# A weight matrix requested earlier and the start of a Fourier-mixing and MLP kernel rearranged around three waits of TensorE

## The chip, the cores and the metric

The kernel runs on one core of one Trainium2 chip. The metric is the device time of one execution in microseconds (us). A profiled execution also gives the span (first to last instruction) and the mean granted clock of TensorE (PE). The span is about 1.8 us shorter than the device time (626.1 against 627.84 us in the profiled run of before).

## The reference, cut to what matters

```python
def _attn_ref(x):                       # x: 8 x 3008 x 256
    X = np.fft.fft(x, axis=1)
    X = np.fft.fft(X, axis=2)
    return X.real.astype(np.float32)

def _moe_ref(x, w_tok1, w_tok2, w_ch1, w_ch2):
    xt = x.transpose(0, 2, 1)
    h = np.maximum(xt @ w_tok1, 0.0) @ w_tok2       # tokens: 3008 -> 256 -> 3008
    u = x + h.transpose(0, 2, 1)
    h2 = np.maximum(u @ w_ch1, 0.0) @ w_ch2         # channels: 256 -> 1536 -> 256
    return u + h2
```

## The kernel before

For each of eight batches the kernel computes the two Fourier transforms as products with generated tables (`fold`, then `z`, `w`, and `y` as the third stage), the token relu (`tok1`), the sum `u` (`tok2`), and the channel MLP (`mm1` with relu, `mm2`). In the traces PE keeps the order in which the kernel emits its instructions, also where it waits: in the changed kernel it idles 0.68 us before a `pw` at 73.32 us, and the two `pc` emitted behind that `pw` start at 73.50. What fills PE while it waits is therefore decided by the order in which the kernel emits work. Python generators give out that work in steps: `take(own, 2)` emits the next two steps of the first batch's front part.

```python
    def filler(n):                      # matmuls whose result nobody reads
        pw = ps_out("filler")
        for _ in range(n):
            nc.tensor.matmul(pw[:, 0:P], lhsT=ident[:], rhs=lrot[:], start=True, stop=True)
    ...
    # the copy of z out of PSUM: copy(1, ...) is VectorE, copy(0, ...) ScalarE
                copy(half == 0 and b > 0 or b == 0 and t0 == 1 and half, zo[:, :, :, t0:t0 + 5], ...)
    ...
        if b == 0:
            yield from rot()
            yield from y(0)
            yield from tok1()           # the token relu uu
            yield from tok2(0)          # pu <- uu, then ut
            for c in (1, 2):
                yield from y(c)
                yield from tok2(c)
    ...
    def mm1(b, c, c1, ct):              # pc <- ut, two halves h
        ...
        for h in range(2):
            nc.tensor.matmul(pc[:, 0:n], lhsT=wc1[:, h, ct * P:(ct + 1) * P],
                             rhs=ut[:, c, h, 0:n], start=(h == 0), stop=(h == 1))
    ...
    take(own, 2)
    take(tu_r, 3)
    filler(8)
    take(own, 2)
    filler(8)
    take(own, 4)                        # z is whole after this
    take(tu_b0, 3)                      # back: pr <- tts, copied by VectorE
    take(tu_b2, 3)                      # back: pr <- tts, copied by ScalarE
    ...
    for k in range(6):
        take(own, 2)                    # two pw
        take(car, 1)                    # one ph <- w1p, w1m
    ...
    NFRONT = 42                         # steps of the next batch's front, spread over the slots
    ...
                while done < NFRONT * (slot + 1 - first) // (71 - first):
                    take(nxt, 1)
                    done += 1
```

The first token matrix is loaded as `w1p` and `w1m` from the POOL queue. It was requested after all generated tables and their memsets, near 10 us.

## Time and profile before

| | before |
|---|---|
| device time, first three runs | 629.15 us (628.19 to 629.95) |
| span of the profiled run | 626.1 us, clock 0.999 |
| PE busy | 609.8 us, 97% |
| PE idle after 44 us, before the last matmul | none that the waits view shows |
| first `prot` / first `po` | 26.32 / 44.95 us |

The page's line of the chain that ended last says who limits the kernel. PE holds 96% of it.

```profile
PE 96%; DVE 2%; DMA 1%; ACT 0%; issue 0%; DVEq 0%
```

The view of PE's waits, longest first, in the kernel before. The columns are: who waited, for whom, us in total, times, longest.

```profile
PE filler L344 <- DVE ident L84: 8.0, 1, 8.0
PE pr L380 <- DVE tts L384: 1.0, 2, 0.8
PE pu L488 <- DVE uu L84: 0.9, 1, 0.9
PE pz L418 <- DVE eo L90: 0.5, 1, 0.5
PE pc L545 <- DVE ut L90: 0.5, 2, 0.3
...
```

The lines shown all lie in the first 37 us. The timeline of PE in the kernel before shows where. The columns are: start, duration, engine, line, operation, result and sources, shapes, count, and the idle time before with its releaser.

```profile
13.51 1.48 PE L371 MATMUL pr<-lrot,tp 128*128 128x128 f16 x12
...
20.04 0.38 PE L380 MATMUL pr<-tts,anti 128*128 128x512 f16 x1 [0.82 <-DVE tts L384]
...
21.32 0.27 PE L442 MATMUL pw<-td,z 128*128 128x257 f16 x1
...
34.60 0.96 PE L488 MATMUL pu<-w2n,uu 128*128 128x512 f16 x3 [0.93 <-DVE uu L84]
35.81 0.38 PE L545 MATMUL pc<-ut,wc 128*128 128x512 f16 x1 [0.26 <-DVE ut L90]
36.41 0.38 PE L545 MATMUL pc<-ut,wc 128*128 128x512 f16 x1 [0.22 <-DVE ut L90]
...
44.95 1.47 PE L575 MATMUL po<-wc,c 128*128 128x256 f16 x12
```

`pw` starts at 21.32 because `back` (`pr`) waits for VectorE's copies. `pu` waits for the token relu. The two halves of the first `pc` wait for the two halves of `ut`.

The table of busy time by window in the kernel before: window, length, busy us and count of PE, PEld, DVE, ACT and POOL, then PE clock, DMA share, GB/s.

```profile
10.00:11.00 1.00, 1.00 (x6) 0.45 (x5) 1.00 (x4) 0.90 (x2) 1.00 (x4) 1.00 1.07 217
11.00:12.00 1.00, 1.00 (x12) 0.93 (x9) 1.00 (x4) 1.00 (x3) 1.00 (x2) 1.00 0.67 53
12.00:13.00 1.00, 0.47 (x6) 0.28 (x5) 1.00 (x5) 1.00 (x2) 1.00 (x3) 1.00 0.86 139
```

The last column falls from 217 to 53 GB/s. The requests for the token rows were nearly served, and those for `w1p` went out only from 10.12 us on, too late to follow without a gap.

### The profile page before, as it was taken

The numbers are of one execution on the slowest core, as the hardware profiler recorded it, in microseconds if no ns is written. First come the engines' busy times: TensorE is split into PE (matmuls) and PEld (weight loads), VectorE is DVE, ScalarE is ACT, GpSimd is POOL, SyncE is SP. The second block draws the span as 40 slices with busy tenths as digits, with TensorE's granted clock in tenths as the row PEclk, the third lists the DMA queues.
The fourth block names the chain that finished last, engine by engine and source line by source line (L and its number), as shares of the span: only waits on it lengthen the run. The fifth ranks groups of instructions, "written<-read, shape, count | busy, mean of one in ns | idle before, by whom it ended". The sixth has DMA issues, their size and how long they took to land.

```text
span 626.1 us, 11728 instructions
## 1 busy us (share of the span) xinstructions
PE 609.8 (97%) x4765; PEld 423.0 (68%) x4765; DVE 343.2 (55%) x730; ACT 291.0 (46%) x571; POOL 170.5 (27%) x231
## 2 busy tenths in 40 slices
PE   4889999999999999999999999999999999999997
PEld 3656676667667676667766776667766677666666
DVE  8768647634664356554665447653466536653343
ACT  8643553554434643365434544356443554344441
POOL 8401890292013900166010850039000000000000
PEclk9999999999999999999999999999999999999999
DMA  8994845428224462426532296242223323332435
GB/s 149 210 157 87 146 81 122 85 60 155 53 52 93 80 135 61 80 52 134 107 69 50 64 153 92 48 94 51 51 52 67 86 51 52 82 68 56 89 64 106
DMA packets 83366, 55.46 MB, mean 89 GB/s; under 512 B 53746, under 2 KB 80050, under 8 KB 82546
## 3 DMA queue, kind: packets, MB, share of 16 engines
q1 hardware_dynamic: 76816, 36.82, 30.0%
q0 software_dynamic: 6176, 17.63, 15.8%
q8 instruction: 37, 0.61, 0.4%
q10 hardware_dynamic: 320, 0.26, 0.2%
q14 instruction: 17, 0.14, 0.1%
HBM read 35.26 MB, written 24.64 MB: 96 GB/s over the span
## 4 chain that ended last, share of the span: by engine, by line
PE 96%; DVE 2%; DMA 1%; ACT 0%; issue 0%; DVEq 0%
PE po L575 39%; PE pc L545 39%; PE pu L488 7%; PE pt L510 3%; PE pz L418 2%; PE py L468 2%; PE pw L442 2%; DMA xm<-in_x_dram,ix 1%; PE pw L444 1%; PE ph L397 0%; PE ph L399 0%; PE filler L344 0%; DVE z L101 0%; DVE ut L90 0%; PE pr L371 0%; DVE eo L90 0%
## 5 line engine op out<-in xcount | busy, mean ns | idle before, releaser
L545 PE MATMUL pc<-ut,wc 128*128 128x512 f16 (+1 forms) x1152 | 306.6, 374 | 0.7 <-DVE ut L90 0.5
L97 ACT ACTIVATE c<-pc 128x512 f16<-128x512 f32 (+1 forms) x384 | 214.2, 587 | 195.8 <-PE pc L545 142.7
L575 PE MATMUL po<-wc,c 128*128 128x256 f16 x2256 | 276.3, 273 | 0.0
L575 PEld LDWEIGHTS <-c 128*128 128x128 f16 x2256 | 220.6, 98 | 63.2
L84 DVE TENSOR_SCALAR c<-pc 128x512 f16<-128x512 f32 (+1 forms) x192 | 129.8, 676 | 98.6 <-PE pc L545 97.8
L545 PEld LDWEIGHTS <-wc 128*128 128x128 f16 x1152 | 103.2, 98 | 69.6 <-issue 4.2
L90 DVE TENSOR_TENSOR osb<-po,uT 128x258 f32<-128x258 f32 (+1 forms) x196 | 71.8, 408 | 125.4 <-PE po L575 122.4
L90 DVE TENSOR_TENSOR ut<-pu,yt 128x512 f16<-128x512 f32 (+1 forms) x96 | 63.6, 672 | 9.7 <-PE pu L488 9.7
L97 ACT ACTIVATE w<-pw 128x257 f16<-128x257 f32 x90 | 34.6, 385 | 50.9 <-PE pw L444 50.9
L90 POOL TENSOR_TENSOR eo<-fa,fb 96x512 f16<-96x512 f16 (+1 forms) x48 | 54.1, 1148 | 0.0
L488 PE MATMUL pu<-w2r,uu 128*128 128x512 f16 (+1 forms) x168 | 50.0, 379 | 0.0
L689 POOL COPY tail<-c 128x768 f16<-128x768 f16 x4 | 3.3, 823 | 170.2 <-ACT c L97 170.2
L687 POOL COPY c<-tail 128x768 f16<-128x768 f16 x4 | 3.3, 823 | 138.9 <-PE po L575 138.9
L90 DVE TENSOR_TENSOR yt<-py,sqy 128x512 f16<-128x512 f32 x48 | 30.9, 685 | 9.5 <-ACT sqy L97 9.5
L488 PEld LDWEIGHTS <-uu 128*128 128x128 f16 x192 | 18.7, 98 | 16.0 <-DVE uu L84 1.3
L90 POOL TENSOR_TENSOR fa<-xp,xm 96x512 f16<-96x512 f16 x24 | 27.5, 1146 | 1.9 <-DMA xm<-in_x_dram,ix 1.9
L101 DVE CAST z<-pz 128x480 f16<-128x480 f32 (+1 forms) x38 | 24.3, 652 | 6.1 <-PE pz L418 5.0
L90 POOL TENSOR_TENSOR fb<-xm,xp 96x512 f16<-96x512 f16 x24 | 27.5, 1146 | 0.0
L97 ACT ACTIVATE z<-pz 128x480 f16<-128x480 f32 x26 | 17.2, 675 | 20.1 <-PE pz L418 19.7
L97 ACT ACTIVATE sqy<-py 128x512 f32<-128x512 f32 x24 | 14.3, 596 | 25.1 <-PE py L468 23.8
L442 PE MATMUL pw<-td,z 128*128 128x257 f16 x96 | 25.6, 273 | 0.0
L90 POOL TENSOR_TENSOR eo<-xp,xm 96x4 f16<-96x4 f16 x24 | 5.2, 217 | 73.0 <-PE pz L432 72.9
(136 smaller groups left out, 338.3 us busy)
## 6 DMA issues: line engine op xcount, KB each, us to landing
out_dram<-osb SPq DMA_DIRECT2D x83, 256.0 KB
xp<-in_x_dram POOLq DMA_DIRECT2D x14, 408.0 KB, 5.2
out_dram<-osb SPq DMA_DIRECT2D x11, 192.0 KB
uT<-ut SPq DMA_TRANSPOSE x96
w2n<-in_moe_w_tok_dram POOLq DMA_DIRECT2D x2, 752.0 KB, 13.2
w1p<-in_moe_w_tok_dram POOLq DMA_DIRECT2D x2, 384.0 KB, 5.4
wc<-in_moe_w_ch_dram POOLq DMA_DIRECT2D x1, 768.0 KB, 16.4
xp<-in_x_dram POOLq DMA_DIRECT2D x2, 272.0 KB
```

The lines of the kernel that those rows point to most:

```text
L84: eng.tensor_scalar(out=out_, in0=in_, scalar1=s1, scalar2=None, op0=op0)
L90: eng.tensor_tensor(out=out_, in0=a, in1=b, op=op)
L97: nc.scalar.activation(out=out_, in_=in_, func=func, scale=scale, **kw)
L101: V.tensor_copy(out=out_, in_=in_)
L418: nc.tensor.matmul(pz[:, 96 * k:96 * k + 96], lhsT=eo[:, t0 + k, c], rhs=t1r, start=True, stop=True)
L442: nc.tensor.matmul(pw[:, 0:257], lhsT=zg[:, 1, g], rhs=td1[:], start=True, stop=False)
L444: nc.tensor.matmul(pw[:, 0:129], lhsT=zg[:, 0, g], rhs=td0[:], start=False, stop=True)
L468: nc.tensor.matmul(py[:, P * k:P * k + P], lhsT=w[:, 4 * c + k, o:o + P], rhs=tab[:, 4 * c + k, :], start=True, stop=True)
L488: nc.tensor.matmul(pu[:, 0:64 * nk], lhsT=uu[:, th, h, :], rhs=w2[:, th, :, 8 * c:8 * c + nk], start=(th == 0), stop=(th == 1))
L510: nc.tensor.matmul(pt[:, o:o + n], lhsT=hw[:, g, c], rhs=w[:, g, w0:w0 + n], start=(g == 0), stop=(g == NG - 1))
L545: nc.tensor.matmul(pc[:, 0:n], lhsT=wc1[:, h, ct * P:(ct + 1) * P], rhs=ut[:, c, h, 0:n], start=(h == 0), stop=(h == 1))
L575: nc.tensor.matmul(po[:, o:o + D], lhsT=c1[:, ct, ks * P:ks * P + P], rhs=wc2[:, ct, :], start=(ct == 0), stop=(ct == NCT - 1))
```

## The change

It has four parts, named by letters from here on.

- **W**: `w1p` and `w1m` are requested right behind the first token rows, from 6.4 us.
- **Z**: `back` is cut up and spread between the `z` steps and the `pw` steps, more `z` copies go to ScalarE, and 12 of 28 fillers go.
- **Y**: the third stage `y` has three steps, and the first two steps of `y(1)` are emitted between the token relu and `tok2(0)`, so that its eight matmuls fill the wait for `uu`. The third step of `y` also raises the number of steps per batch, so `NFRONT` becomes 45.
- **H**: the first three `pc` of the first chunk run all their first halves, then all their second halves.

```diff
+    load_w1p()
     ts(mask[:, 0:1], pcol[:], float(NQ), AT.is_lt, eng=G)
     ts(top[:], pcol[:], float(KR - 1), AT.is_lt, eng=G)
     tt(mask[:, 1:2], xicol[:], top[:], AT.mult, eng=G)
+    load_w1m()
+    (memsets of w1m, e128, td1 moved here too; loads and memsets removed at the old place)
@@ z copies
-                copy(half == 0 and b > 0 or b == 0 and t0 == 1 and half, zo[:, :, :, t0:t0 + 5],
+                copy(half == 0 and b > 0, zo[:, :, :, t0:t0 + 5],
-            copy(1, zo, pz[:, 0:96].rearrange("p (u k) -> p u k", u=4))
+            copy(b > 0 or half, zo, pz[:, 0:96].rearrange("p (u k) -> p u k", u=4))
@@ y
             act(sq[:], ps[1][:])
+            yield
@@ front, b == 0
+            y1 = y(1)
+            next(y1)
+            next(y1)
+            yield
             yield from tok2(0)
-            for c in (1, 2):
-                yield from y(c)
-                yield from tok2(c)
+            yield from y1
+            yield from tok2(1)
+            yield from y(2)
+            yield from tok2(2)
@@ mm1: cts=range(3) for the first call, loops over the three pc inside each half (cut)
@@ order of the start
-    filler(8)
+    filler(4)
     take(own, 2)
-    filler(8)
+    take(tu_b0, 2)
     take(own, 4)
-    take(tu_b0, 3)
-    take(tu_b2, 3)
+    take(tu_b0, 1)
     for k in range(6):
         take(own, 2)
+        take(tu_b2, 1 if 0 < k < 4 else 0)
         take(car, 1)
@@
-    NFRONT = 42
+    NFRONT = 45
```

(The counts of `take(own, ...)` and the slots in `own_at`, which follow from the new steps, are cut.)

More of the change, by code (lines that the diff above doesn't have):

```diff
@@ L158, with load_w1p, load_w1m @@
     tw23, q25 = pvec("tw23"), pvec("q25")
+    def load_w1p():
+        for i in range(2):
+            gdma(w1p[64 * i:64 * i + 64, :, :].rearrange("p (c g) d -> p c (g d)", c=3),
+                 dram(w1_t, 4 * i * DTOK, [[NQ * DTOK, 64], [8 * DTOK, 3], [1, 4 * DTOK]]))
+    def load_w1m():
+        for i in range(2):
+            h = slice(64 * i, 64 * i + 64)
+            n = 3 - i
+            gdma(w1m[h, 0:4 * n, :].rearrange("p (c g) d -> p c (g d)", c=n),
+                 dram(w1_t, (24 + 4 * i) * DTOK,
+                      [[NQ * DTOK, 64], [8 * DTOK, n], [1, 4 * DTOK]]))
+        gdma(w1m[64:128, 8:11, :].rearrange("p g d -> p (g d)"),
+             dram(w1_t, 44 * DTOK, [[NQ * DTOK, 64], [1, 3 * DTOK]]))
     V.memset(tw23[:], TWO23)
@@ L179 @@
     top, acol = pvec("top"), pvec("acol")
+    ixc = const.tile([P, 2], I32, tag="ixc")
+    cfeat = pvec("cfeat")
+    load_w1p()
     ts(mask[:, 0:1], pcol[:], float(NQ), AT.is_lt, eng=G)
@@ L182 @@
     tt(mask[:, 1:2], xicol[:], top[:], AT.mult, eng=G)
-    ixc = const.tile([P, 2], I32, tag="ixc")
-    cfeat = pvec("cfeat")
+    load_w1m()
+    G.memset(w1m[64:128, 11, :], 0.0)
+    G.memset(e128[:], 0.0)
+    G.memset(td1[:, 0:130], 0.0)
+    G.memset(td1[0:1, 0:128:2], 0.5)
+    G.memset(td1[0:1, 1:129:2], -0.5)
     ts(cfeat[:], pcol[:], 1.0, AT.is_ge, 128.0, AT.mult, eng=G)
@@ L271 @@
     sin(td1[:, 130:257], md[:, 129:256])
-    G.memset(e128[:], 0.0)
-    G.memset(w1m[64:128, 11, :], 0.0)
-    G.memset(td1[:, 0:130], 0.0)
-    G.memset(td1[0:1, 0:128:2], 0.5)
-    G.memset(td1[0:1, 1:129:2], -0.5)
-    for i in range(2):
-        gdma(w1p[64 * i:64 * i + 64, :, :].rearrange("p (c g) d -> p c (g d)", c=3),
-             dram(w1_t, 4 * i * DTOK, [[NQ * DTOK, 64], [8 * DTOK, 3], [1, 4 * DTOK]]))
-    for i in range(2):
-        h = slice(64 * i, 64 * i + 64)
-        n = 3 - i
-        gdma(w1m[h, 0:4 * n, :].rearrange("p (c g) d -> p c (g d)", c=n),
-             dram(w1_t, (24 + 4 * i) * DTOK,
-                  [[NQ * DTOK, 64], [8 * DTOK, n], [1, 4 * DTOK]]))
-    gdma(w1m[64:128, 8:11, :].rearrange("p g d -> p (g d)"),
-         dram(w1_t, 44 * DTOK, [[NQ * DTOK, 64], [1, 3 * DTOK]]))
     ts(acol[:], pcol[:], -1.0, AT.mult, 127.0, AT.add, eng=G)
@@ L538, in front, with mm1 @@
                 yield from tok2(c)
-    def mm1(b, c, c1, ct):
+    def mm1(b, c, c1, ct, cts=None):
         ut = state[b]["ut"]
         n = min(CW, S - CW * c)
-        pc = ps_mm("pc")
+        cts = cts or (ct,)
+        pcs = [ps_mm("pc") for _ in cts]
         for h in range(2):
-            nc.tensor.matmul(pc[:, 0:n], lhsT=wc1[:, h, ct * P:(ct + 1) * P],
-                             rhs=ut[:, c, h, 0:n], start=(h == 0), stop=(h == 1))
-        if ct % 3:
-            act(c1[:, ct, 0:n], pc[:, 0:n], func=AFT.Relu)
-        else:
-            ts(c1[:, ct, 0:n], pc[:, 0:n], 0.0, AT.max)
+            for pc, ct in zip(pcs, cts):
+                nc.tensor.matmul(pc[:, 0:n], lhsT=wc1[:, h, ct * P:(ct + 1) * P],
+                                 rhs=ut[:, c, h, 0:n], start=(h == 0), stop=(h == 1))
+        for pc, ct in zip(pcs, cts):
+            if ct % 3:
+                act(c1[:, ct, 0:n], pc[:, 0:n], func=AFT.Relu)
+            else:
+                ts(c1[:, ct, 0:n], pc[:, 0:n], 0.0, AT.max)
     tail1 = const.tile([P, NCT, 64], FP16, tag="tail1")
@@ L637 @@
         take(own, 2)
+        take(tu_b2, 1 if 0 < k < 4 else 0)
         take(car, 1)
-    take(own, 3)
+    take(own, 4)
     take(car, 6)
-    take(own, 4)
+    take(own, 5)
     setup.close()
@@ L645 @@
     w2v[1] = w2r[:]
-    NFRONT = 42
-    own_at = {0: 2, 2: 1, 3: 1, 12: 1, 15: 1, 18: 1, 21: 1, 24: 1, 27: 1, 30: 1, 33: 1,
+    NFRONT = 45
+    own_at = {1: 1, 2: 1, 4: 1, 12: 1, 15: 1, 18: 1, 20: 1, 22: 1, 24: 1, 27: 1, 30: 1, 33: 1,
               36: 1, 39: 1}
@@ L660 @@
                 slot = NCT * c + ct
-                mm1(b, c, c1, ct)
+                if b == 0 and slot < 3:
+                    if slot == 0:
+                        mm1(b, c, c1, ct, range(3))
+                else:
+                    mm1(b, c, c1, ct)
                 if ct == 4:
```

## The prediction

> **What bounds the kernel.** The page gives TensorE 97% busy at a granted clock of 1.0, and the chain of waits is 96% PE. In the table of busy time by window, PE has no idle time from 44 us to the last matmul (622 us); 4.0 us of output DMA follow. So only the first 44 us can be shortened. Of them PE is idle about 12.4 us, 8.0 before anything can run. The rest, from the timeline of PE:
> - 18.8 to 21.3 us: `back` waits for three VectorE copies (2.08 us), which wait behind the stage-one copies `z`; the first `pw` starts at 21.32, although `z` is whole at 19.46.
> - 33.2 to 34.6: `pu` waits for the token relu `uu` (0.93 idle).
> - 35.2 to 36.4: `pc` waits for the two halves of `ut`.
> DMA is saturated near 200 GB/s from 2.3 to 43 us, except 11 to 12.7 us, where it falls to about 0 to 100 GB/s: `w1p` was requested only at 10.1, the token rows were finished.
>
> **What the change does.** No arithmetic is removed but 12 fillers.
> 1. `w1p`, `w1m` requested from about 6.4 instead of 10.1. [...] Missing bytes of the gap at 205 GB/s: 1.0 us (estimate). The last `w1m` piece landed near 21.1 before (second piece 20.6, by landings), so near 20.1.
> 2. `mask` moves behind two DMA issues (1.38 us): ready near 9.2. VectorE needs it for `t1n` and 0.7 us more before the fold; the fold waits for tokens until 9.99 anyway. Delay 0 to 0.4.
> 3. `back` is split and interleaved, both last `z` copies go to ScalarE: `z` whole near 18.7 to 19.2, `pw` starts there, about 2.3 earlier. But `ph` then meets `w1m` at 20.1, and the loop gets 3 `pr` (0.22 each) and 3 ScalarE copies (0.54 each) more: about 5.3 us of PE or 5.1 of ScalarE. `prot` starts near 25.0 instead of 26.32: gain 1.3.
> 4. `y(1)`'s eight matmuls (0.43) fill the wait for `uu`; three first-half `pc` (0.65) fill the wait for the second `ut`. Afterwards VectorE's queue (relu 0.6, `yt` 1.2, `ut` 0.6) rules until `pc` of ct 6: gain 0.8.
> 5. From then on PE is full; the third yield per `y` reorders VectorE work only, with no idle PE to gain or lose: 0.
>
> **Predicted time.** 629.15 - 1.3 - 0.8 = 627.05, say 627.0 us (0.35%), 8 in 10 between 625.2 and 628.7. Over 2% faster would need 12.6 us, more than the start can give: 0.01; over 2% slower 0.01; within 0.98.
>
> **What would show it.** DMA at 11 to 12.7 us near 200 GB/s; first `pw` at 18.7 to 19.3 with a PE wait for DMA `w1m` (to about 20.1) before the first `ph`; `prot` near 25.0; PE wait for `uu` under 0.5; the first `po` near 42.9 instead of 44.95; from there to the end the same length within 0.3 us.
>
> **What would make it wrong.** `w1p` sharing the engines with the second token gather and delaying the fold; [...] ScalarE as new limit of the `pw` loop; run-to-run scatter of 1.8 us, as large as the gain.

Two passages are cut. One gave a rule for the order of transfers in a queue as the reason why `w1p` and `w1m` would run behind the token rows; without it that order was assumption. The other was a risk for which no trace here gives a measure. No term of the forecast goes with them: 629.15 - 1.3 - 0.8 = 627.05. The "near 200 GB/s" is 185 to 212 GB/s in the trace of before, at a busy share of 0.99 to 1.18, over the stretches from 2.3 to 43 us without the gap.

## The result, and the profile after

| | before | changed |
|---|---|---|
| device time, six runs | 628.67 us (627.39 to 630.14) | 626.53 us (626.34 to 628.33) |
| span, changed runs at clock 1.000 | | 624.6, 624.6, 624.7, 624.8 |
| span, changed runs at clock 0.997 | | 626.5, 626.6 |

The ratio is 0.9974, with a 95% interval from 0.9951 to 0.9996. A ratio is worked out from the runs of both kernels, so it is not quite the ratio of the medians. The time lies inside the predicted range, and the medians differ by 2.14 us, as forecast. The table's last two rows already show that this is not the whole story: the six runs of the changed kernel fall in two groups, and the clock sorts them.

The profiled run was one of the slower group. Its waits of PE:

```profile
PE filler L350 <- DVE ident L84: 8.7, 1, 8.7
PE pw L448 <- DVE z L101: 0.7, 1, 0.7
PE pw L448 <- ACT z L97: 0.6, 1, 0.6
...
PE ph L405 <- DMA w1m<-in_moe_w_tok_dram: 0.5, 1, 0.5
...
PE pu L495 <- DVE uv L90: 0.4, 1, 0.4
...
```

Its timeline of PE, in the places shown of before (line numbers have shifted):

```profile
13.84 0.83 PE L377 MATMUL pr<-lrot,tp 128*128 128x128 f16 x12
...
19.17 0.27 PE L448 MATMUL pw<-td,z 128*128 128x257 f16 x1 [0.56 <-ACT z L97]
...
20.50 0.37 PE L405 MATMUL ph<-w1m,tts 128*128 128x256 f16 x1 [0.51 <-DMA w1m<-in_moe_w_tok_dram]
...
34.81 1.29 PE L495 MATMUL pu<-w2n,uu 128*128 128x512 f16 x4 [0.44 <-DVE uv L90]
36.36 1.46 PE L559 MATMUL pc<-ut,wc 128*128 128x512 f16 x6 [0.26 <-DVE ut L90]
...
45.05 1.47 PE L590 MATMUL po<-wc,c 128*128 128x256 f16 x12
```

Four things are as intended: `pw` starts at 19.17 instead of 21.32, `ph` meets `w1m`, the wait of `pu` falls from 0.93 to 0.44 us (and now ends with `uv`, the step before the token relu), and the six `pc` run as one group. Yet the first `po` comes at 45.05, no earlier than before, where 42.9 was predicted. In the table by window the DMA gap is filled, and the PE clock shows the main reason why the gain is missing in this run (besides, VectorE began the fold of the tokens 0.55 us later than in the trace of before, at 10.54 us):

```profile
11.00:12.00 1.00, 1.00 (x7) 0.66 (x6) 1.00 (x4) 1.00 (x3) 0.87 (x5) 1.00 0.99 180
...
16.55:19.96 3.41, 2.15 (x23) 1.41 (x24) 3.31 (x10) 2.77 (x6) 2.33 (x4) 1.00 1.12 206
19.96:23.37 3.41, 2.90 (x16) 2.02 (x15) 0.96 (x3) 1.71 (x4) 2.78 (x4) 0.50 1.15 227
```

From 19.96 to 23.37 us the clock is 0.50, right where the `pw` and `ph` loop runs. The trace of before has no such stretch. It pays in another place: its twelve `pr` at 13.51 take 1.48 us against 0.83 in the changed trace, because PE still ran at a slow rate then. Both traces start at this rate: their first twelve fillers, of the same 128x128 shape, take 1.46 us. It ended where the clock records begin. In the trace of before they begin only at 17.23 us, with the full clock, and ten `pz` take 1.00 us at 15.64 and 0.59 at 17.27; those of the changed kernel begin at 13.13. (They are in the packed traces. The views print 1.00 where there is no record, so the 1.00 in the lines above that end before these times says nothing.)

The third new item is a wait that did not exist before, `pw` for a VectorE copy of `z`, 0.7 us. It is at 73 us, in what was the full part:

```profile
72.40 0.18 PE L433 MATMUL pz<-t1n,eo 96*128 96x24 f16 x1
72.43 0.17 PE L436 MATMUL pz<-cms,e 96*128 96x24 f16 x1
72.45 0.19 PE L438 MATMUL pz<-t1b,eo 96*128 96x72 f16 x1
73.32 0.28 PE L448 MATMUL pw<-td,z 128*128 128x257 f16 x1 [0.68 <-DVE z L101]
```

### The profile page after: what moved, and what is told of

It reads as the page before. It is cut to its first block, busy times and chain, and to the rows that moved or that the text cites. A ratio compares the mean times of both kernels' runs of the same rounds, so it can differ in the third digit from the quotient of the medians. Undisturbed runs are those within 1.5% of the kernel's fastest.

```text
span 626.6 us, 11701 instructions
## 1 busy us (share of the span) xinstructions
PE 608.9 (97%) x4753; PEld 420.9 (67%) x4753; DVE 344.8 (55%) x728; ACT 293.2 (47%) x573; POOL 170.4 (27%) x231
## 4 chain that ended last, share of the span: by engine, by line
PE 95%; DMA 2%; DVE 1%; POOL 1%; ACT 0%; issue 0%; DVEq 0%
PE po L590 39%; PE pc L559 39%; PE pu L495 7%; PE pt L517 3%; PE pw L448 2%; DMA w1m<-in_moe_w_tok_dram 2%; PE py L474 2%; PE pz L424 1%; PE pw L450 1%; PE ph L405 0%; PE ph L403 0%; POOL xm L109 0%; DVE ix L86 0%; POOL w1p L106 0%; POOL w1m L106 0%
## 5 line engine op out<-in xcount | busy, mean ns | idle before, releaser
L97 ACT ACTIVATE z<-pz 128x480 f16<-128x480 f32 (+1 forms) x28 | 18.2, 686 | 26.7 <-PE pz L424 26.7
```

The source lines that it names most:

```text
L97: nc.scalar.activation(out=out_, in_=in_, func=func, scale=scale, **kw)
```

## The experiments

Theory A is the prediction: the four parts shorten the start by 1.3 (W and Z) and 0.8 us (Y and H). To this came two theories from the trace: C, the new wait at 73 us is made by `NFRONT` 45; and D, the half-clock stretch, called the dip from here on, is caused by too little matmul work in the 3.41 us before it, so the kernel can avoid it. (A clock window means such a stretch of 3.41 us from here on. The section on the dip shows where the windows lie.) Their rivals are that the wait is made up elsewhere, and that the dip is chance. Twelve kernels ran, each beside the kernel before on the same chip. All twelve gave correct results. p1 to p4 ran on one chip, p5 to p8 on a second and p9 to p12 on a third. The kernel before took 625.6 to 625.7, 625.5 to 625.7 and 625.4 to 625.6 us on them in its runs at clock 1.000, so a comparison across these groups can be off by about 0.2 us. "Clean" means a run at clock 1.000 or 0.999, "dip" one at 0.997 or lower.

### p1_again: the changed kernel once more

No edit.

> The changed kernel once more, for a second profile and the shares of its runs. Theory A (the start is shorter by the four parts, and a dip of the TensorE clock to half for 3.4 us spoils some runs): runs fall in two groups, span near 624.7 us at a granted clock of 1.000 and near 626.5 us at 0.997, nothing between; in a profile without the dip prot starts near 25.0 to 25.5 and the first po near 43.0. Theory B (the clock in the records is a side matter and the scatter is start-up chance alone): times spread evenly over 2 us and don't go with the clock.

Measured: spans 626.0, 626.2, 626.2, 626.4 at 0.997, and 625.0 at 1.000. The ratio is 0.9996 (0.9983 to 1.0009): in these rounds the change brought nothing, as four of its five runs dipped, and three of the eleven of before. Of these, before had 625.6 to 625.7 in its five runs at 1.000. Its three runs at 0.999 took 626.2 to 626.4, like its profiled run (626.1 at 0.999), which kept the slow rate of the start until 17.23 us. That the three did so too is likely and not shown. They are left out wherever runs at 1.000 are compared. The two groups are confirmed, and the median is set by how many runs dip. No clean profile of the changed kernel was caught; p7 gives one.

### p2_noW: without part W

```diff
-    load_w1p()            # behind the token rows
-    load_w1m()
+    load_w1p()            # at the old place, after the tables
+    load_w1m()
```

> The change without its first part: w1p and w1m requested at their old place, near 10 us. Theory A: first pw still near 18.7 to 19.2, but PE then waits for w1m until about 21.1 to 21.6 before ph can go on (0.5 us with the early request), so it is 0.8 to 1.2 us slower than the changed kernel in runs of the same clock. Rival: the gain comes from the rest alone, and the early request is worth under 0.3 us.

Measured: 625.3 in the one clean run against 624.6 to 625.0 of the changed kernel, four dips (626.1 to 626.9). In the profile, which is of the clean run, PE waited for `w1m` until 20.57 us, not until 21.1 to 21.6 as expected, and the loss is 0.3 to 0.7 us instead of 0.8 to 1.2. One clean run is too little; p10 repeats it without dips.

### p3_noZ: without part Z

```diff
-    filler(4)
+    filler(8)
     take(own, 2)
-    take(tu_b0, 2)
+    filler(8)
     take(own, 4)
-    take(tu_b0, 1)
+    take(tu_b0, 3)
+    take(tu_b2, 3)
@@ and the z copies as before; take(tu_b2, ...) goes from the loop (cut)
```

> The change without the split of back and without the z copies on ScalarE (16 fillers again). Theory A: the first pw starts near 21.3 us as before, no wait for w1m, and it is 1.0 to 1.5 us slower than the changed kernel in runs of the same clock; with 16 fillers the half-clock dip near 20 us does not come. Rival: the w1m landing is the limit anyway, so it is under 0.5 us slower.

Measured: 625.6, 625.6, 625.7 clean, two dips (626.4, 626.7). Against the changed kernel's 624.6 to 625.0, part Z is worth 0.6 to 1.1 us at equal clock, a little less than expected. The first `pw` starts at 20.80. My guess that 16 fillers in their old places prevent the dip was wrong: the profiled run has one from 19.11 us.

### p4_noY: without part Y

```diff
-            y1 = y(1)
-            next(y1)
-            next(y1)
-            yield
             yield from tok2(0)
-            yield from y1
-            yield from tok2(1)
+            yield from y(1)       # after tok2(0), as before; y in two steps, NFRONT 42
+            yield from tok2(1)
```

> The change without y(1) filling the wait for the token relu (and without the third yield of y). Theory A: the wait of pu for uu is 0.9 us instead of 0.44, and it is 0.3 to 0.5 us slower. Rival: VectorE's queue rules until pc of ct 6, so moving 0.43 us of PE work changes nothing: under 0.15 us.

Measured: 625.1, 625.1, 625.2 clean, three dips. The wait for `uu` is 0.92 us again. From `prot` (26.36) to the first `po` (45.38) it takes 19.02 us; the changed kernel takes 18.21 (26.84 to 45.05) and the kernel before 18.63. So Y is worth 0.8 us beside H, and H alone makes this stretch 0.4 longer. The total loses less than 0.8, as this kernel doesn't have the new wait at 73 us: from the first `po` to the end it takes 581.1 us, like before, and the changed kernel 581.5.

### p5_noH: without part H

```diff
-                if b == 0 and slot < 3:
-                    if slot == 0:
-                        mm1(b, c, c1, ct, range(3))
-                else:
-                    mm1(b, c, c1, ct)
+                mm1(b, c, c1, ct)
```

> The change without the first chunk's halves apart. Theory A (prediction): pc of the first half has no more work to fill the wait for the second half of ut, 0.3 to 0.4 us slower in runs at the same clock. Rival: VectorE's queue rules up to ct 6, so at most 0.1 us. Seen before: from prot to the first po 18.63 us in the kernel before, 18.21 with both parts, 19.02 with the halves apart but no filled relu wait; this run gives the fourth corner.

Measured: `prot` (26.27) to the first `po` (44.43) 18.16 us, against 18.21 with H. Clean spans 624.7 and 624.8, no difference; the other four runs dipped (625.9 to 626.5). The fourth corner is in: neither 18.63, Y alone 18.16, H alone 19.02, both 18.21. Part H is worth nothing beside Y, and alone it costs 0.4.

### p6_pace: the extra step of y only where it is used

```diff
             act(sq[:], ps[1][:])
-            yield
+            if b == 0:
+                yield
@@
-    NFRONT = 45
+    NFRONT = 42
```

> The changed kernel with y's third yield only for the first batch and NFRONT 42 again. Theory C: the third yield set NFRONT to 45, the first batch then takes its eighth and ninth step in one slot, and pw waits 0.7 us for the z copy (seen near 73 us in all four kernels with 45, not in the two with 42); so this wait goes, the stretch from the first po to the end falls from 581.5 to 581.1 us, and runs at the same clock are 0.3 to 0.5 us shorter. Rival: the wait is made up elsewhere, no difference.

Measured: the wait is gone. PE's timeline of this kernel at the same place has the two `pc` back between `pz` and `pw`:

```profile
72.08 0.19 PE L438 MATMUL pz<-t1b,eo 96*128 96x72 f16 x1
72.11 0.60 PE L560 MATMUL pc<-ut,wc 128*128 128x512 f16 x2
73.02 0.27 PE L448 MATMUL pw<-td,z 128*128 128x257 f16 x1
```

From the first `po` (44.68) to the end (625.8) it takes 581.1 us instead of 581.5, as theory C asks. The dipping runs are 625.6 to 626.0 against 625.9 to 626.6 of the changed kernel and p5. The one clean run is 624.5. The cause can be counted from the code: of the steps of the next batch that are taken during the first batch, step 8 is the last `pz` and step 9 the first `pw`. With 45 steps over 40 slots, the floor of 45·n/40 is 7 at n = 7 and 9 at n = 8, so both fall in one slot with no `pc` between them; with 42 it is 8 and then 9.

### p7_fill: fillers in the waits of the start

```diff
     take(tu_b0, 2)
-    take(own, 4)
+    filler(4)
+    take(own, 1)
+    filler(4)
+    take(own, 1)
+    filler(4)
+    take(own, 2)
     take(tu_b0, 1)
+    filler(8)
```

> The changed kernel with 20 fillers put into the waits of PE between 16 and 19.2 us. Theory D: the half-clock stretch of 3.4 us that starts between 19.1 and 20.0 in the dipping runs comes from a window with too little matmul work before it (0.7 to 1.34 us of columns in 3.41 us); the fillers add 1.07 us, so no run has a clock of 0.997 and all spans are near 624.7 to 625.0. Rival (dip is chance of the chip or of temperature, not of the work): 2 to 4 of 5 runs at 0.997 as with the changed kernel.

Measured: no dip in six runs, spans 624.5 to 624.8, device time 626.48 us (626.30 to 626.58), ratio 0.9976 (0.9963 to 0.9989). In the same rounds the kernel before dipped in 5 of 11 runs. The fillers cost nothing, as the spans are those of the changed kernel's clean runs. The timeline of PE is the clean one that was missing:

```profile
18.61 0.27 PE L448 MATMUL pw<-td,z 128*128 128x257 f16 x1
...
19.80 0.27 PE L405 MATMUL ph<-w1m,tts 128*128 128x256 f16 x1 [0.37 <-DMA w1m<-in_moe_w_tok_dram]
...
24.83 0.18 PE L457 MATMUL prot<-w,lrot 128*128 128x12 f16 x1 [0.16 <-ACT w L97]
...
43.03 1.47 PE L590 MATMUL po<-wc,c 128*128 128x256 f16 x12
```

### p8_best: fillers, pace, and a better order of the w1m pieces

```diff
             gdma(w1m[h, 0:4 * n, :] ...)
+            if i == 0:
+                gdma(w1m[64:128, 8:11, :] ...)   # 96 KB, needed by the first ph
-        gdma(w1m[64:128, 8:11, :] ...)           # was last, behind 256 KB that later ph need
@@ and the edits of p6 and p7
```

> Pace as in p6, fillers as in p7, and the third piece of w1m (96 KB) requested before the second (256 KB), which only later matmuls need. Theory: the 0.5 us wait of ph for w1m at 20 us goes too; no dips; spans 0.7 to 1.0 us below the changed kernel's clean runs (624.7 to 625.0), so near 624.0. Rival: the ScalarE copies limit the pw loop, the w1m wait is then made up, and it only gets p6's and p7's gain.

Measured: six runs, all with a span of 624.2 and a device time of 625.96 to 625.99 us. The ratio is 0.9968 (0.9955 to 0.9981). The wait for `w1m` is gone from the waits view. The expected 624.0 was missed by 0.2. Against p7 that is 0.3 to 0.6 us, about what p6 gives alone; so the piece order may be worth little, as its rival said. It was not run alone.

### p9_before_fill: the kernel before, with fillers

```diff
     filler(8)
-    take(own, 4)
+    filler(4)
+    take(own, 1)
+    take(own, 1)
+    filler(4)
+    take(own, 1)
+    filler(3)
+    take(own, 1)
     take(tu_b0, 3)
+    filler(10)
     take(tu_b2, 3)
```

> The kernel before with 21 more fillers in its own waits of PE between 15.6 and 20 us, so that the clock stays up. If the dip comes from too little matmul work in a clock window (theory D), no run is at 0.997 and all spans are near 625.7, the clean span of the kernel before: that alone would take away most of the scatter, and the change compared at equal clock is worth 1.0 us (625.7 against 624.6 of the changed kernel with fillers). Rival: fillers help only the changed schedule, 4 of 11 runs dip as before.

Measured: no dip in five runs (spans 625.2, 625.2, 625.3, 625.3, 626.1), while the kernel before dipped in 4 of 9 in the same rounds. So the remedy does not depend on the change. The expected spans near 625.7 came out 0.4 lower in four runs; why the fifth took 626.1 at clock 1.000 is open. Its timeline of PE gives a clean base for the change:

```profile
20.57 0.27 PE L442 MATMUL pw<-td,z 128*128 128x257 f16 x1
...
25.57 0.18 PE L451 MATMUL prot<-w,lrot 128*128 128x12 f16 x1 [0.16 <-ACT w L97]
...
44.20 1.47 PE L575 MATMUL po<-wc,c 128*128 128x256 f16 x12
```

### p10_best_noW, p11_best_noZ, p12_best_noH: one part less, without dips

p10 is p8 with the loads at the old place and in the old piece order; p11 is p8 with part Z undone and the fillers placed as in p9; p12 is p8 with part H undone. The edits are those of p2, p3 and p5. p10 thus undoes two things at once, the early request and the order of the pieces. Part Y has no such run; it rests on p4 and on the lengths from `prot` to the first `po`.

> The best kernel so far (fillers, pace; 624.2 us in every run) with w1p and w1m requested at the old place. Without dips the early request is measured alone: ph waits for w1m until about 20.5 to 21.5 us instead of not at all, so span 624.9 to 625.6. Rival: under 0.3 us.

> The best kernel with back in one piece before the pw loop and the z copies as before, with fillers in its waits. pw can't start before the three VectorE copies of back: near 20.4 to 21.3 us; the early w1m then has no use. Theory A: span 625.0 to 625.4 (about 1 us worse). Rival: under 0.3 us worse, as the loop is three pr shorter.

> The best kernel with the first chunk's halves not apart. In profiles prot to the first po took 18.16 us without and 18.21 with the halves apart, so I expect 624.1 to 624.3, no difference: VectorE's queue rules there (relu, yt, ut), not the order of the pc matmuls. The prediction's share for it (0.3 to 0.4 us) would show 624.5 to 624.6.

| kernel | clean spans | median | dips |
|---|---|---|---|
| p9: before, fillers | 625.2 to 626.1 | 625.3 | 0 of 5 |
| p7: changed, fillers | 624.5 to 624.8 | 624.7 | 0 of 6 |
| p8: with pace and piece order | 624.2 in all | 624.2 | 0 of 6 |
| p10: p8 without W | 624.9 to 625.4 | 625.1 | 0 of 5 |
| p11: p8 without Z | 624.9 to 625.3 | 625.2 | 0 of 5 |
| p12: p8 without H | 623.7 to 624.1 | 624.1 | 0 of 5 |

W and Z need each other. Without Z, or without W and the order of the pieces, the kernel loses 0.9 to 1.0 us and is back near p9. In p10 PE waits 0.7 us for `w1m`, and `prot` starts at 25.74. In p11 `prot` starts at 25.57, exactly where it does in p9, with the weights long there. In p8 it starts at 24.84. The lines of PE's timeline, of p8, p10 (two) and p11:

```profile
24.84 0.18 PE L458 MATMUL prot<-w,lrot 128*128 128x12 f16 x1 [0.16 <-ACT w L97]
20.70 0.27 PE L405 MATMUL ph<-w1m,tts 128*128 128x256 f16 x1 [0.73 <-DMA w1m<-in_moe_w_tok_dram]
25.74 0.18 PE L457 MATMUL prot<-w,lrot 128*128 128x12 f16 x1 [0.16 <-ACT w L97]
25.57 0.18 PE L458 MATMUL prot<-w,lrot 128*128 128x12 f16 x1 [0.16 <-ACT w L97]
```

p10 and p11 still have part Y. Its 0.4 us shows in the spans of the profiled runs of p11 and p9 (624.9 and 625.3), but the medians differ by 0.1 only, so the scatter of the start hides much of it. H is again worth nothing. p8 ran on another chip than p9 to p12; the 0.2 us between these chips, applied to p8, would make the losses 1.1 to 1.2 and change none of these conclusions. p8 and p12 beat both kernels; their device times are 625.96 and 625.91 us.

### What makes the dip

The clock records of the changed trace last 6.83, 3.41 and 604.16 us (the last of these to 627.53 us), and the full-clock record of the trace of before lasts 607.57 us. These are 2, 1, 177 and 178 times 3.413 us, so the clock changed at the borders of windows of that length. Each of the six dips lasted 3.41 us at 0.50. They began at 19.96, 19.16, 19.11, 19.45, 18.85 and 19.27 us in the changed kernel, p1, p3, p4, p5 and p6, so the borders don't keep a fixed distance from the start of the kernel. After the last matmul the clock records drop once more: in the changed trace it ends at 622.7 us, and the drop comes at 627.53. In all six traces this drop comes 607.57 us after the start of the dip, which is 178 windows. The borders of the runs that did not dip are counted back from their drop at the end in the same steps. That is an estimate, and the trace of before fits it: its first record starts 178 windows before its drop at 624.80.

For each profile, the table has the matmul work in the window before a border between 17.8 and 21.5 us. Work means columns at 2.4 per ns, an estimate from the spacing of `pc` in the traces of both kernels (0.216 us for 512 columns, which is 2.37 per ns, rounded; 2.37 would make every entry 1% longer). A matmul counts with the columns that fall inside the window when they follow its start at this rate.

| kernel | window, us | work, us | clock after it |
|---|---|---|---|
| changed | 16.55 to 19.96 | 1.28 | 0.50 |
| p1 | 15.74 to 19.16 | 0.92 | 0.50 |
| p3 | 15.70 to 19.11 | 1.13 | 0.50 |
| p4 | 16.04 to 19.45 | 1.34 | 0.50 |
| p5 | 15.44 to 18.85 | 1.06 | 0.50 |
| p6 | 15.85 to 19.27 | 1.02 | 0.50 |
| before | 17.23 to 20.64 | 1.36 | 1.00 |
| p2 | 14.58 to 17.99 | 1.53 | 1.00 |
| p2 | 17.99 to 21.41 | 1.46 | 1.00 |
| p7 | 14.66 to 18.07 | 2.25 | 1.00 |
| p11 | 14.46 to 17.88 | 2.07 | 1.00 |
| p8 | 15.53 to 18.94 | 2.03 | 1.00 |
| p10 | 15.76 to 19.18 | 2.16 | 1.00 |
| p9 | 16.09 to 19.50 | 2.25 | 1.00 |
| p12 | 16.31 to 19.72 | 2.34 | 1.00 |

Up to 1.34 us the clock fell, from 1.36 us on it held. That the two groups nearly touch rests on the kernel before alone: one `pr` of 512 columns starts 0.01 us before its border, and counted whole it makes 1.56. (The 0.7 in the expectation of p7 was a miscount that left out one `pr`.) The busy share of the views does not sort the windows as the columns do: PE was busy for 1.80 us in p2's second window, which held, and for 2.15 in that of the changed kernel, which did not. The four last rows are the strongest evidence: their borders lie inside the range in which all the others dipped, and the fillers are what differs. The line of p12 in the table by window, to set beside the changed kernel's window at 16.55 above:

```profile
16.32:19.73 3.41, 3.02 (x42) 2.43 (x40) 3.18 (x10) 2.71 (x7) 3.11 (x6) 1.00 1.13 208
19.73:23.14 3.41, 3.41 (x34) 2.73 (x32) 2.30 (x5) 3.41 (x9) 2.10 (x4) 1.00 1.11 218
```

Over all runs with a recorded clock, kernels with added fillers dipped in 0 of 32, the changed kernel and its variants without them in 24 of 39, the kernel before in 12 of 31 (once at 0.993, so by estimate for two windows or more, as one of 3.41 us at 0.50 takes 0.003 off the mean of a run). Theory D stands. The changed kernel alone dipped in 6 of 11. A larger share than before would fit its sparser stretch, but the two counts are too small to show it.

## Why the prediction was right, and where its steps were not

The time was right: 627.0 predicted, 626.53 measured, inside 625.2 to 628.7. The way to it holds in part only. Two dip-free profiles of single runs, p9 for before and p7 for the changed kernel, give the account at equal clock:

| stretch | before (p9) | changed (p7) | gain | predicted |
|---|---|---|---|---|
| start to `prot` | 25.57 | 24.83 | 0.74 | 1.3 |
| `prot` to first `po` | 18.63 | 18.20 | 0.43 | 0.8 |
| first `po` to the end | 581.1 | 581.5 | -0.4 | 0 |
| span | 625.3 | 624.5 | 0.8 | 2.1 |

- **Step 1 (DMA), right in kind.** The gap at 11 to 12 us is filled, 180 GB/s instead of 53. The last needed piece of `w1m` let PE go on at 19.80 in p7 and 20.50 in the profile of the changed kernel; 20.1 was predicted. The token fold was not visibly delayed by the early request, as the prediction had assumed (fold start 9.99 us before, 10.04 in p7, 10.54 in the changed profile, 10.27 in p9; p10, without the early request, has 10.58). The gain was smaller than the estimated 1.0 us: PE got past its wait for `w1m` at 19.80 to 20.50 us with the early request (p7, p4, changed) and at 20.57 and 20.70 without it (p2, p10).
- **Step 2 (`mask`), right.** VectorE had no wait for it in the changed profile; the fold waited 0.84 us for the tokens after that work was done.
- **Step 3 (`back`, `z`), mechanism right, size wrong.** `pw` at 18.6, the wait for `w1m`, and `prot` at 24.83 (predicted 25.0) came as said. The base was wrong: "instead of 26.32" was read from one trace that had stayed at the slow rate of the start until 17.23 us, where the thirteen other traces left it between 11.05 and 13.13 (by the first clock record of each). In p9 `prot` starts at 25.57. The gain is 0.74, not 1.3. It is not the scatter of the fold: p8, whose fold starts at 10.26 like that of p9, has `prot` at 24.84. That the slow rate makes the whole of the 0.75 us between 26.32 and 25.57 is argued, not shown, as p9 has its fillers besides and no profile of the kernel before alone without the slow start was caught. Of the last three `z` copies only two went to ScalarE; the very last stayed on VectorE (0.59 us in the changed profile), against the words of the step.
- **Step 4 (Y and H), half wrong.** Filling the wait for `uu` is worth 0.4 to 0.5 (18.63 to 18.16). "Three first-half `pc` fill the wait for the second `ut`" adds nothing. It removes that wait (0.22 us at 36.41 in the trace of before), and PE waits for ScalarE's copies `c` twice, 0.25 us each, where it does so once without H (changed trace against p5). The prediction had named a limit in this place, though VectorE's queue; the two savings cannot be added.
- **Step 5 ("the third yield reorders VectorE work only: 0"), wrong.** It changed `NFRONT`, and the rounding of the pace put two dependent steps side by side: 0.68 us of wait, 0.4 us of time.
- **Not foreseen: the dip.** It costs 1.0 to 2.0 us in the runs of the changed kernel that it hits (within the same rounds: 624.6 to 624.8 clean against 626.5 and 626.6, and 625.0 against 626.0 to 626.4), more than the change brings. The prediction named the scatter but not its cause, and it counted the removed fillers only as work saved.

So why did the measured medians differ by 2.1 us? At equal clock the change is worth 0.6 to 1.0 us: 0.8 in the account above (where p7's profiled run is its fastest), 0.6 between the medians of p9 and p7, and 1.0 between p7's median of 624.7 and the 625.7 of the runs of before at 1.000 on the same chip. The rest is the mix of runs: four of the six changed runs were clean, while the median of the six of before, 628.67, lies above the 627.2 to 627.5 that its clean runs have in the later rounds. Their clocks were not kept, so that part is inferred. In the rounds of p1 the mix went the other way and the ratio was 0.9996. The right total came from summing terms that were too large, and from a lucky draw of clocks.

## What to carry to other kernels

When a gain is below half a per cent, sort the runs by granted clock before reading any median, and look in the profile for where the clock falls. Dense matmul work in the start-up phase is not only throughput: here 20 useless matmuls in waits that existed anyway cost nothing (p7's spans are 624.5 to 624.8, the clean ones of the changed kernel 624.6 to 625.0) and took the dips away (0 of 6 runs against 6 of 11). And when the number of steps in a paced schedule changes, check which steps now share a slot.

## What the traces leave open

- The clock fell with no long gap. The longest idle gap that the trace shows in the changed kernel's window from 16.55 to 19.96 us is 0.56 us, and PE counts as busy in 2.15 of 3.41 us. What separates the cases is the work in one window: with at most 1.34 us of columns the clock fell, with at least 1.36 us it held (estimates). Whether the rule is a sum of columns, and how sharp it is, stays open.
- What ends the slow rate of the start, and why it lasted until 17.23 us in the trace of before and until 13.13 us in that of the changed kernel, was not tested.
- One VectorE instruction on a 128x16 tile, the same in all kernels and issued at 1.85 us, took 0.91 us in some profiles (before, p7, p9, p12) and 1.69 or 1.70 in others (p1, changed). It ended at 2.76 or at 3.54 us, just behind the end of POOL's DMA issue (2.64) or of its following iota (3.51), and PE's first matmul then started at 7.94 to 7.97 or at 8.71 to 8.72. What decides between the two was not tested.
